# P times V in the attention stage: 16 products of 128 rows and 130 columns in place of 32 of 64 rows and 65 columns

## The chip, the cores and the metric

The kernel runs on one core of one Trainium2 chip. The metric is the time of one execution on the device, in microseconds (us), and the median of several runs is compared. All inputs lie in the device's memory (HBM) when it starts. Host work that lays the arrays out beforehand (`layout`) is not timed.

## The reference

Two stages run one after the other. First comes windowed attention over 8 batches, 8 heads, 576 positions and head size 64. Heads 0 to 3 see the last 32 positions; heads 4 to 7 see every fourth of the last 128:

```python
scores = np.where(masks[None], scale * np.matmul(q, k.transpose(0, 1, 3, 2)), -1e9)
attn = np.exp(scores - np.max(scores, axis=-1, keepdims=True))
attn = attn / (np.sum(attn, axis=-1, keepdims=True) + 1e-09)
attn_out = np.matmul(attn, v)
```

Its output, as 4608 tokens of 512 numbers, goes into a mixture of 16 experts in 4 groups of 4. Each token picks its group by the largest group logit and then its expert by the largest logit within the group, and gets `g_w * e_w * (relu(x @ w1[e]) @ w2[e])`.

## The kernel before

**Attention.** The positions are cut into blocks of 64, and two batches go together: a step `n` (0 to 35, constant `NT`) is one block of all 8 heads of two batches. The dilated heads are sorted by position modulo 4 beforehand, so that each 32 queries see only their own and the previous 32 keys, whatever the head. A step has 8 slots `bb*4 + c` (batch `bb`, head group `c`), each with two head parities or kinds `w`, and two query halves `a`. So one step holds 16 small attentions of 64 queries.

The loop `for s in range(NT + 3)` (L899) is a pipeline: iteration `s` has on TensorE (PE) `scores(s)` (one product with the mask at L263, then 16 products q times k at L275), `transpose_p(s-1)` (four transposes of the probabilities, L298), `av(s-2)` (P times V, L308) and `transpose_x(s-3)` (L360). VectorE (DVE) does the maximum (L285), the subtraction (L286), the reciprocal (L334) and the normalisation (L336). ScalarE (ACT) does the exponential (L291) and the copies out of PSUM (L299, L362, L364). The order on PE, ACT, DVE and SP (the queue that issues the loads and stores) is the order in which the code calls them (`tc.manual_schedule`, L898); GpSimd (POOL) is placed by the framework. The loads run ahead: q and k four steps, v three steps (L920 to L922). Into the same loop the routing of finished batch pairs (`route`, L367), the loads and splits of expert weights (`run(wq)`, L945) and, in the last iterations, early work of the experts are woven, so many pieces per iteration by a budget (`spend`, L250).

**P times V before** (`av`, L301). After the transpose, `pt` holds for each `c` the 128 rows (w, key): rows 0 to 63 belong to `w = 0`, rows 64 to 127 to `w = 1`. For each `c`, `w`, `bb`, `a` one product takes 64 rows of `pt` (32 columns, the queries) and 64 rows of V (65 columns: 64 values and a constant that gives the sum of the probabilities): 32 products of a 64-row, 32-column tile of the array. In the profile each float32 product appears as two matrix instructions and two weight loads, so a step shows 64 pairs. For `a = 1` V is read from `vt` (as loaded), for `a = 0` from `vs`, a copy that `shift_v` (L123) makes on POOL: all of `vt[n]`, then the 32 rows at 0 and at 64 from the block before, three instructions of 520 columns. `vt` and `vs` are rotating buffers of one pool (NV = 5, NVS = 4), 2,080 bytes per partition each; a load of V is one DMA of 128 rows (L121).

**After attention** the pools of it are closed (`att.close()`, L954), and the tiles of the second weight set (`wb`), the expert inputs and others take their place in SBUF and wait for whatever lay there. From then on the experts' two layers (L759, L818) run over 16 experts.

The functions that the change touches, and what calls them:

Of the kernel before, what the change touches and what calls it, by code (L numbers as in the profile page):

```python
# [8 lines left out]
F32 = mybir.dt.float32  # L9
# [3 lines left out]
AF = mybir.ActivationFunctionType  # L13
ALU = mybir.AluOpType
# [3 lines left out]
P = 128  # L18
B, H, S, D = 8, 8, 576, 64
# [5 lines left out]
NJ = S // 64  # L25
NT = NBP * NJ
# [4 lines left out]
SCALE = 0.125  # L31
# [17 lines left out]
NQ, NK, NV, NVS, NPT = 4, 6, 5, 4, 2  # L49
# [15 lines left out]
def moe_attention_kernel(ctx, tc, q, k, v, cmask, wgate, wpack, out):  # L65
    nc = tc.nc
# [11 lines left out]
    id32 = cp.tile([P, P], F32, name="id32")  # L78
# [16 lines left out]
    att = ExitStack()  # L95
    apool = lambda name, bufs=1, **kw: att.enter_context(tc.tile_pool(name=name, bufs=bufs, **kw))
    psA = apool("psA", 1, space=PSUM)
    vp = apool("vp", NV)
    qp = apool("qp", NQ)
    kr = apool("kp").tile([P, 2, 2 * NK, 8, 32], F32, name="kr")  # L100
    pt = [apool(f"pt{i}").tile([P, 4, P], F32, name=f"pt{i}") for i in range(NPT)]
    qb, vt, vs, st, dd, oo, dn = {}, {}, {}, {}, {}, {}, {}
# [14 lines left out]

    def load_v(n):
        if n < NT:
            vt[n] = vp.tile([P, 8, 65], F32, name="vt")  # L120
            nc.sync.dma_start(vt[n], v[n])  # L121

    def shift_v(n):  # L123
        vs[n] = vp.tile([P, 8, 65], F32, name="vs", bufs=NVS)
        nc.gpsimd.tensor_scalar(vs[n], vt[n], 1.0, 1.0, ALU.mult, ALU.mult)
        for r in range(2):
            odd = slice(64 * r, 64 * r + 32)
            if n % NJ == 0:
                nc.gpsimd.memset(vs[n][odd], 0.0)
            else:  # L130
                nc.gpsimd.tensor_scalar(vs[n][odd], vt[n - 1][odd], 1.0, 1.0, ALU.mult, ALU.mult)

    nc.vector.memset(kr[:, :, 0 : NK + 1 : NK], 0.0)
    nc.sync.dma_start(masks[:, 0:2], cm[:, 0:2])
# [7 lines left out]
    load_k(1, 1, 1)  # L142
    load_q(1)
    load_v(0)
    nc.sync.dma_start(masks[:, 2:], cm[:, 2:])
    load_k(2, 0)
    load_k(2, 1)
    load_q(2)
    load_v(1)
    load_q(3)  # L150
    load_v(2)

    ones = cp.tile([P, P], BF16, name="ones")
# [63 lines left out]
    ap = apool("ap", 3)  # L217
# [69 lines left out]
        dd[n] = d  # L287

    def softexp(n):
        p = ap.tile([P, 8, 64], F32, name="p", bufs=2)  # L290
        nc.scalar.activation(p, dd.pop(n), AF.Exp, scale=SCALE)  # L291
        st[n] = p

    def transpose_p(n):
        p = st.pop(n)
        t = psT.tile([P, 4, P], F32, name="t", tag="t")
        for c in range(4):
            nc.tensor.transpose(t[:, c, :], p[:, 2 * c : 2 * c + 2, :].rearrange("p a b -> p (a b)"), id32)  # L298
        nc.scalar.copy(pt[n % NPT], t)  # L299

    def av(n):  # L301
        o = psA.tile([P, 2, 512], F32, name="o", tag="o")
        for c in range(4):
            for w in range(2):
                for bb in range(2):
                    for a in range(2):
                        j = bb * 2 + a
                        nc.tensor.matmul(  # L308
                            o[32 * j : 32 * j + 32, w, c * 65 : c * 65 + 65],
                            pt[n % NPT][64 * w : 64 * w + 64, c, 32 * j : 32 * j + 32],  # L310
                            (vs, vt)[a][n][64 * w : 64 * w + 64, bb * 4 + c, :],
                            start=True,
                            stop=True,
                        )
        oo[n] = o
        den = ap.tile([P, 2, 4], F32, name="den")
        ov = o[:, :, 0:260].rearrange("p k (s c) -> p k s c", c=65)
        nc.scalar.activation(den, ov[:, :, :, 64], AF.Copy, bias=1e-9 / SX)
        dn[n] = den
# [10 lines left out]
    def normalise(n):  # L330
        o = oo.pop(n)
        ov = o[:, :, 0:260].rearrange("p k (s c) -> p k s c", c=65)
        den = dn.pop(n)
        nc.vector.reciprocal(den, den)  # L334
        x = ap.tile([P, 4, 2, 64], F32, name="x", bufs=5)
        nc.vector.tensor_tensor(  # L336
            x.rearrange("p s w c -> p w s c"),
            ov[:, :, :, 0:64],
            den.unsqueeze(3).broadcast_to([P, 2, 4, 64]),
            ALU.mult,  # L340
        )
        st[n] = x
# [549 lines left out]

    start = []
    shift_v(0)
    shift_v(1)
    man = ExitStack()
    ET = mybir.EngineType
    man.enter_context(tc.manual_schedule(engines={ET.PE, ET.Activation, ET.DVE, ET.SP}))  # L898
    for s in range(NT + 3):  # L899
# [3 lines left out]
        if 0 <= s - 1 < NT:  # L903
            transpose_p(s - 1)
        if 0 <= s - 2 < NT:
            av(s - 2)
        if s < NT:
            softexp(s)
        if 0 <= s - 2 < NT:
            if ripe:  # L910
                gate.clear()
            normalise(s - 2)
        if start:
            n = start.pop()
# [13 lines left out]
        if s + 2 < NT:  # L928
            shift_v(s + 2)
# [219 lines left out]
def layout(q, k, v, moe_w_group, moe_w_expert, moe_w1, moe_w2):  # L1149
    import ml_dtypes  # L1150
    import numpy as np

    def seqs(a):
        a = np.asarray(a)
        d = a[:, 4:].reshape(B, 4, CLS, 4, D).transpose(0, 1, 3, 2, 4).reshape(B, 4, S, D)
        return np.stack([a[:, :4], d], axis=1).reshape(NBP, 2, 2, 2, 2, S, D)

    qs, ks, vs = seqs(q), seqs(k), seqs(v)
    qa = qs.reshape(NBP, 2, 2, 2, 2, 3, 3, 2, 32, D)
    qa = qa.transpose(0, 5, 6, 9, 4, 1, 2, 3, 7, 8).reshape(NT, P, 512)  # L1160
    kpad = np.concatenate([np.zeros_like(ks[..., :32, :]), ks], axis=-2).reshape(*ks.shape[:5], 19, 32, D)
    kg = [kpad[..., [2 * j + 2, 2 * j + 1], :, :] for j in range(NJ)]
    ka = np.stack([a.transpose(0, 4, 7, 5, 1, 2, 3, 6) for a in kg], axis=1).reshape(NT // 2, 2, 2, 64, 2, 256)
    ka = ka.transpose(0, 2, 3, 4, 1, 5).reshape(NT // 2, 2, 64, 1024)
    vw = vs.reshape(NBP, 2, 2, 2, 2, 3, 3, 2, 32, D)[..., ::-1, :, :]
    va = vw.transpose(0, 5, 6, 4, 7, 8, 1, 2, 3, 9).reshape(NT, P, 8, D)
    va = np.concatenate([va, np.full_like(va[..., :1], 1.0 / SX)], axis=-1)

    cmask = np.full((2, 2, 32, len(MASKS), 2, 64), -1e9, np.float32)
    for mi, J in enumerate(MASKS):  # L1170
        for a in range(2):
            for qq in range(32):
                i = 64 * J + 32 * a + qq
                for kd in range(2):
                    start = 0 if kd == 0 else (i // CLS) * CLS
                    for kk in range(64):
                        half = (1 - a) * (kk // 32 - 1) - a * (kk // 32)
                        j = i - qq + 32 * half + kk % 32
                        if 0 <= i - j < 32 and j >= start:
                            cmask[:, a, qq, mi, kd, kk] = 0.0  # L1180
    cmask = cmask.reshape(P, -1).astype(ml_dtypes.bfloat16)
    wg = np.concatenate([np.asarray(moe_w_group), np.asarray(moe_w_expert).transpose(1, 0, 2).reshape(DM, 16)], axis=1)
    wg = np.concatenate([wg, np.zeros((DM, 12), wg.dtype)], axis=1)
    wgate = wg.reshape(4, P, 32).transpose(1, 0, 2).reshape(P, -1)
    tok = np.arange(NTOK).reshape(NCHK, P).T
    row = tok // S * S + tok % S % 4 * CLS + tok % S // 4
    pair = 2.0 * (row - PAIR2 // 2 * (tok // (PAIR2 // 2) + 1))
    wgate = np.concatenate([wgate, 2.0 * (row - NTOK), pair], axis=1).astype(np.float32)
    w1 = np.asarray(moe_w1).reshape(NE, 4, P, FF).transpose(0, 2, 1, 3).reshape(NE, P, 4 * FF)
    w2 = np.asarray(moe_w2).reshape(NE, 8, P, DM).transpose(0, 2, 1, 3).reshape(NE, P, 8 * DM)  # L1190
    wpack = np.concatenate([w1, w2], axis=2).reshape(NE * P, 8192)
    c = np.ascontiguousarray
    return dict(q=c(qa), k=c(ka), v=c(va), cmask=c(cmask), wgate=c(wgate), wpack=c(wpack))
# [21 lines left out]
```

## Time and profile before

| | us |
|---|---|
| median of 3 runs | 597.36 |
| lowest and highest run | 597.07, 603.14 |
| the profiled execution, its own time | 598.75 |
| its span, first to last instruction | 597.0 |

The profile holds one execution. Its first part gives the busy time of each engine over the span: PE 561.4 us, its weight loads (PEld) 393.8, DVE 389.5, ACT 326.4, POOL 241.9. Shares over the whole span mix two stages: up to about 172 us the attention steps run, and from about 194 us to the end the experts alone. Matrix instructions overlap in the array and their ends are modelled, so the start of the next group tells more of the pace than a duration does. "Issue" as a releaser means that an engine waited for nothing that the profile shows. Queue q8 and q14 carry the engines' own instructions.

### The profile page before, as it was taken

The page shows a single profiled execution, that of the slowest core. Times are in us where ns is not written, and L with a number is a line of the kernel's source. Part 1 is how long each engine was busy: PE and PEld are TensorE (multiplying, and loading weights), DVE is VectorE, ACT ScalarE, POOL GpSimd, SP SyncE. Part 2 cuts the span into 40 slices and gives each one's busy share as a digit, 9 for nine tenths or more (in the row PEclk, how much of TensorE's full clock was granted, in tenths as well). Part 3 has the DMA queues.
Part 4 walks back from the last instruction along what each step waited for, and adds up shares of the span by engine and source line. Part 5 has one row for each costly group of instructions (what it writes and reads, how often), then busy time and mean ns, then how long its engine had stood idle before and what let it go on. Part 6 is the DMA issues. An engine that isn't in the chain of part 4 may idle for free.

```text
span 597.0 us, 18617 instructions
## 1 busy us (share of the span) xinstructions
PE 561.4 (94%) x7588; PEld 393.8 (66%) x7588; DVE 389.5 (65%) x804; ACT 326.4 (55%) x650; POOL 241.9 (41%) x313
## 2 busy tenths in 40 slices
PE   5888989889698999999999999999999999999995
PEld 3665767566485757765657566666767757767873
DVE  5664876988957833784778695565745766766720
ACT  2554665775555624774455546455655755656521
POOL 4644473636714605161415153442623503423411
PEclk9999999989999999999999999999999999999998
DMA  7998797898473227885677576756867578777300
GB/s 227 307 287 259 230 288 243 285 368 293 99 262 104 80 66 280 284 262 164 198 207 240 176 236 193 223 182 212 250 220 240 197 219 287 234 242 247 94 28 31
DMA packets 48313, 127.52 MB, mean 214 GB/s; under 512 B 7629, under 2 KB 8531, under 8 KB 48226
## 3 DMA queue, kind: packets, MB, share of 16 engines
q1 hardware_dynamic: 40466, 105.33, 55.8%
q0 software_dynamic: 7760, 20.99, 10.2%
q8 instruction: 61, 1.00, 0.7%
q14 instruction: 26, 0.21, 0.1%
HBM read 107.40 MB, written 19.22 MB: 212 GB/s over the span
## 4 chain that ended last, share of the span: by engine, by line
PE 67%; issue 3%; DVE 2%; ACT 1%; POOL 0%; POOLq 0%; ACTq 0%
PE y L818 32%; PE a L759 31%; PE pt L740 3%; DVE mv L505 1%; PE lt_ps L377 0%; PE tx L360 0%; PE o L308 0%; POOL out L779 0%; PE rp L685 0%; PE tb_ps L524 0%; DVE wb1l L641 0%; PE t L298 0%; ACT wb1h L644 0%; ACT room L766 0%; ACT off L243 0%
## 5 line engine op out<-in xcount | busy, mean ns | idle before, releaser
L709 POOL DMA_INDIRECT xr<-xd,sent x80 | 94.5, 1181 | 33.7 <-issue 21.8
L818 PEld LDWEIGHTS <-hh 128*128 128x128 f16 (+14 forms) x960 | 67.3, 99 | 57.6 <-issue 2.5
L779 POOL DMA_INDIRECT out<-yr,sent x30 | 31.0, 1032 | 179.2 <-ACT yr L792 152.7
L767 DVE SCALAR_TENSOR_TENSOR hl<-a,hh 128x256 f16<-128x256 f32 (+14 forms) x136 | 57.1, 422 | 64.1 <-ACT hh L766 64.0
L766 ACT ACTIVATE hh<-a 128x256 f16<-128x256 f32 (+14 forms) x136 | 51.7, 385 | 50.3 <-PE a L759 49.7
L759 PE MATMUL a<-xh,wb1h 128*128 128x256 f16 (+7 forms) x288 | 76.6, 270 | 0.0
L759 PE MATMUL a<-xh,wb1l 128*128 128x256 f16 (+7 forms) x288 | 76.5, 269 | 0.0
L759 PE MATMUL a<-xl,wb1h 128*128 128x256 f16 (+7 forms) x288 | 76.5, 269 | 0.0
L742 DVE TENSOR_TENSOR xl<-pt,xh 128x512 f16<-128x512 f32 (+14 forms) x42 | 24.6, 590 | 73.9 <-ACT xh L741 73.9
L759 PE MATMUL a<-xh,wa1h 128*128 128x186 f16 (+7 forms) x256 | 70.8, 277 | 0.0
L759 PE MATMUL a<-xl,wa1h 128*128 128x186 f16 (+7 forms) x256 | 70.7, 277 | 0.0
L759 PE MATMUL a<-xh,wa1l 128*128 128x186 f16 (+7 forms) x256 | 70.7, 277 | 0.0
L792 ACT ACTIVATE yr<-y,cs 128x512 f32<-128x512 f32 (+4 forms) x30 | 20.7, 688 | 88.7 <-PE y L818 59.5
L759 PEld LDWEIGHTS <-wa1h 128*128 128x128 f16 x640 | 59.0, 98 | 11.5 <-issue 0.3
L759 PEld LDWEIGHTS <-wb1h 128*128 128x128 f16 x576 | 54.3, 98 | 9.6 <-issue 0.2
L818 PE MATMUL y<-wb2h,hh 128*128 128x512 f16 (+7 forms) x272 | 59.7, 305 | 0.0
L818 PE MATMUL y<-wb2l,hh 128*128 128x512 f16 (+7 forms) x272 | 59.5, 304 | 0.0
L818 PE MATMUL y<-wb2h,hl 128*128 128x512 f16 (+7 forms) x272 | 59.5, 304 | 0.0
L818 PE MATMUL y<-wa2h,hh 128*128 128x512 f16 (+7 forms) x208 | 56.8, 331 | 0.0
L818 PE MATMUL y<-wa2h,hl 128*128 128x512 f16 (+7 forms) x208 | 56.6, 330 | 0.0
L818 PE MATMUL y<-wa2l,hh 128*128 128x512 f16 (+7 forms) x208 | 56.6, 330 | 0.0
L818 PEld LDWEIGHTS <-hl 128*128 128x128 f16 (+14 forms) x480 | 34.4, 99 | 25.1
(190 smaller groups left out, 1227.8 us busy)
## 6 DMA issues: line engine op xcount, KB each, us to landing
w<-wpack SPq DMA_DIRECT2D x128, 512.0 KB, 4.8
vt<-v SPq DMA_DIRECT2D x36, 260.0 KB, 4.7
qb<-q SPq DMA_DIRECT2D x36, 256.0 KB, 4.7
xd<-x SPq DMA_DIRECT2D x72, 128.0 KB, 4.2
kr<-k SPq DMA_DIRECT2D x34, 256.0 KB, 5.1
xr<-xd,sent POOLq DMA_INDIRECT x80, 4.5
kr<-k SPq DMA_DIRECT2D x4, 128.0 KB, 3.0
out<-yr,sent POOLq DMA_INDIRECT x30, 3.8
```

The lines of the kernel that those rows point to most:

```text
L505: nc.vector.scalar_tensor_tensor(mv[:, t], high.rearrange("p e k -> p (e k)").unsqueeze(1).broadcast_to([P, 4, NE * NK4]), hl[:, 1, t0 + t ...
L709: nc.gpsimd.indirect_dma_start(out=xr[:, 256 * h : 256 * h + 256], out_offset=None, in_=xd[0:known].rearrange("n (h c) -> (n h) c", h=2), ...
L740: nc.tensor.transpose(pt[:, c, 0:n], xr[0:n, c * P : c * P + P], id32[0:n, 0:n])
L742: nc.vector.tensor_tensor(xl[:, :, t * P : t * P + n], pt[:, :, 0:n], xh[:, :, t * P : t * P + n], ALU.subtract)
L759: nc.tensor.matmul(a[:, 0:cap], ww[:, c * FF + f * P : c * FF + f * P + P], xx[:, c, 0:cap], start=(i == 0), stop=(i == len(mm) - 1),)
L766: nc.scalar.activation(hh[:, f, 0:cap], a[:, 0:cap], AF.Relu)
L767: nc.vector.scalar_tensor_tensor(hl[:, f, 0:cap], a[:, 0:cap], 0.0, hh[:, f, 0:cap], ALU.max, ALU.subtract)
L779: ins = nc.gpsimd.indirect_dma_start(out=out.rearrange("n (g c) -> (n g) c", g=g), out_offset=bass.IndirectOffsetOnAxis(ap=at, axis=0), in ...
L792: nc.scalar.activation(yr[0:n, :], yp[0:n, :], AF.Copy, scale=cs[0:n, t : t + 1])
L818: nc.tensor.matmul(yp[P // g * j : P // g * j + n, 0 : DM // g], h[:, f, t * P : t * P + n], ww[:, f * DM + DM // g * j : f * DM + DM // g ...
```

## The change

- The probabilities are written by `softexp` with the two `w` interleaved (`[P, 4, 64, 2]`), so that after the transpose row `2*key + w` of `pt` belongs to parity `w`.
- V lies in fixed tiles of 128 rows and 2 x 520 columns. Half `w` holds values on the rows of parity `w` alone; the other rows of that half are zero. Zeros are written once per `vt` tile, by an ACT instruction of 1,040 columns; `vs` takes them over with its copies.
- `load_v` issues two DMAs, one per parity, of 64 rows each, in place of one of 128 rows. The bytes are the same.
- `shift_v` issues two POOL instructions of 64 rows and 1,040 columns in place of one of 128 rows and two of 32 rows, of 520 columns each.
- `av` issues 16 products of 128 rows, 32 columns and 130 moving columns (65 per parity).
- PSUM's layout of the output, and the view through which `normalise` writes it, follow; the host's layout of V follows.

```diff
--- before.py
+++ after.py
@@ -95,7 +95,7 @@
     att = ExitStack()
     apool = lambda name, bufs=1, **kw: att.enter_context(tc.tile_pool(name=name, bufs=bufs, **kw))
     psA = apool("psA", 1, space=PSUM)
-    vp = apool("vp", NV)
+    vp = [[apool(f"v{k}{i}").tile([P, 2, 520], F32, name=f"v{k}{i}") for i in range(n)] for k, n in enumerate((NV, NVS))]
     qp = apool("qp", NQ)
     kr = apool("kp").tile([P, 2, 2 * NK, 8, 32], F32, name="kr")
     pt = [apool(f"pt{i}").tile([P, 4, P], F32, name=f"pt{i}") for i in range(NPT)]
@@ -117,18 +117,22 @@
 
     def load_v(n):
         if n < NT:
-            vt[n] = vp.tile([P, 8, 65], F32, name="vt")
-            nc.sync.dma_start(vt[n], v[n])
+            vt[n] = vp[0][n % NV]
+            if n < NV:
+                nc.scalar.activation(
+                    vt[n].rearrange("p w n -> p (w n)"), id32[:, 0:1].broadcast_to([P, 1040]), AF.Copy, scale=0.0
+                )
+            for w in range(2):
+                nc.sync.dma_start(vt[n][w:P:2, w], v[n, w:P:2].rearrange("p s c -> p (s c)"))
 
     def shift_v(n):
-        vs[n] = vp.tile([P, 8, 65], F32, name="vs", bufs=NVS)
-        nc.gpsimd.tensor_scalar(vs[n], vt[n], 1.0, 1.0, ALU.mult, ALU.mult)
-        for r in range(2):
-            odd = slice(64 * r, 64 * r + 32)
-            if n % NJ == 0:
-                nc.gpsimd.memset(vs[n][odd], 0.0)
-            else:
-                nc.gpsimd.tensor_scalar(vs[n][odd], vt[n - 1][odd], 1.0, 1.0, ALU.mult, ALU.mult)
+        vs[n] = vp[1][n % NVS]
+        odd, even = slice(0, 64), slice(64, P)
+        nc.gpsimd.tensor_scalar(vs[n][even], vt[n][even], 1.0, 1.0, ALU.mult, ALU.mult)
+        if n % NJ == 0:
+            nc.gpsimd.memset(vs[n][odd], 0.0)
+        else:
+            nc.gpsimd.tensor_scalar(vs[n][odd], vt[n - 1][odd], 1.0, 1.0, ALU.mult, ALU.mult)
 
     nc.vector.memset(kr[:, :, 0 : NK + 1 : NK], 0.0)
     nc.sync.dma_start(masks[:, 0:2], cm[:, 0:2])
@@ -287,31 +291,32 @@
         dd[n] = d
 
     def softexp(n):
-        p = ap.tile([P, 8, 64], F32, name="p", bufs=2)
-        nc.scalar.activation(p, dd.pop(n), AF.Exp, scale=SCALE)
+        p = ap.tile([P, 4, 64, 2], F32, name="p", bufs=2)
+        d = dd.pop(n).rearrange("p (c w) k -> p c w k", w=2)
+        nc.scalar.activation(p.rearrange("p c k w -> p c w k"), d, AF.Exp, scale=SCALE)
         st[n] = p
 
     def transpose_p(n):
         p = st.pop(n)
         t = psT.tile([P, 4, P], F32, name="t", tag="t")
         for c in range(4):
-            nc.tensor.transpose(t[:, c, :], p[:, 2 * c : 2 * c + 2, :].rearrange("p a b -> p (a b)"), id32)
+            nc.tensor.transpose(t[:, c, :], p[:, c].rearrange("p k w -> p (k w)"), id32)
         nc.scalar.copy(pt[n % NPT], t)
 
     def av(n):
         o = psA.tile([P, 2, 512], F32, name="o", tag="o")
         for c in range(4):
-            for w in range(2):
-                for bb in range(2):
-                    for a in range(2):
-                        j = bb * 2 + a
-                        nc.tensor.matmul(
-                            o[32 * j : 32 * j + 32, w, c * 65 : c * 65 + 65],
-                            pt[n % NPT][64 * w : 64 * w + 64, c, 32 * j : 32 * j + 32],
-                            (vs, vt)[a][n][64 * w : 64 * w + 64, bb * 4 + c, :],
-                            start=True,
-                            stop=True,
-                        )
+            for bb in range(2):
+                for a in range(2):
+                    j = bb * 2 + a
+                    vv = (vs, vt)[a][n].rearrange("p w (s c) -> p w s c", c=65)
+                    nc.tensor.matmul(
+                        o[32 * j : 32 * j + 32, c // 2, c % 2 * 130 : c % 2 * 130 + 130],
+                        pt[n % NPT][:, c, 32 * j : 32 * j + 32],
+                        vv[:, :, bb * 4 + c],
+                        start=True,
+                        stop=True,
+                    )
         oo[n] = o
         den = ap.tile([P, 2, 4], F32, name="den")
         ov = o[:, :, 0:260].rearrange("p k (s c) -> p k s c", c=65)
@@ -334,7 +339,7 @@
         nc.vector.reciprocal(den, den)
         x = ap.tile([P, 4, 2, 64], F32, name="x", bufs=5)
         nc.vector.tensor_tensor(
-            x.rearrange("p s w c -> p w s c"),
+            x.rearrange("p (k s) w c -> p k (s w) c", k=2),
             ov[:, :, :, 0:64],
             den.unsqueeze(3).broadcast_to([P, 2, 4, 64]),
             ALU.mult,
@@ -1163,7 +1168,7 @@
     ka = np.stack([a.transpose(0, 4, 7, 5, 1, 2, 3, 6) for a in kg], axis=1).reshape(NT // 2, 2, 2, 64, 2, 256)
     ka = ka.transpose(0, 2, 3, 4, 1, 5).reshape(NT // 2, 2, 64, 1024)
     vw = vs.reshape(NBP, 2, 2, 2, 2, 3, 3, 2, 32, D)[..., ::-1, :, :]
-    va = vw.transpose(0, 5, 6, 4, 7, 8, 1, 2, 3, 9).reshape(NT, P, 8, D)
+    va = vw.transpose(0, 5, 6, 7, 8, 4, 1, 2, 3, 9).reshape(NT, P, 8, D)
     va = np.concatenate([va, np.full_like(va[..., :1], 1.0 / SX)], axis=-1)
 
     cmask = np.full((2, 2, 32, len(MASKS), 2, 64), -1e9, np.float32)
```

## Rows read from the trace of the kernel before

**Rows 1.** The page: busy time (instructions); instruction queue (packets, MB, share).

```profile
PE 561.4 (94%) x7588; PEld 393.8 (66%) x7588; DVE 389.5 (65%) x804; ACT 326.4 (55%) x650; POOL 241.9 (41%) x313
...
q8 instruction: 61, 1.00, 0.7%
```

**Rows 2.** Windows: bounds, length, PE, PEld, DVE, ACT, POOL, clock, DMA, GB/s.

```profile
16.83:52.53 35.70, 30.40 (x951) 22.20 (x946) 21.87 (x64) 18.60 (x48) 19.54 (x33) 1.00 0.91 288
52.53:104.06 51.53, 48.34 (x1376) 36.00 (x1374) 36.85 (x77) 31.16 (x80) 27.04 (x51) 1.00 0.82 251
104.06:131.77 27.71, 23.16 (x650) 17.02 (x648) 24.96 (x51) 20.80 (x51) 15.26 (x26) 0.94 0.93 319
131.77:172.00 40.23, 33.09 (x883) 24.95 (x880) 32.44 (x73) 25.05 (x65) 22.40 (x33) 0.96 0.71 223
194.00:597.00 403.00, 396.90 (x3350) 271.86 (x3346) 248.90 (x480) 214.65 (x370) 139.07 (x123) 1.00 0.61 196
```

**Rows 3.** Timeline of PE in one undisturbed step: start, us, instruction.

```profile
18.16 0.66 PE L298 MATMUL t<-id,p 128*128 128x128 f32 x4
...
18.75 0.24 PE L308 MATMUL o<-vs,pt 64*32 64x65 f32 x1
...
19.54 0.66 PE L360 MATMUL tx<-id,x 128*128 128x128 f32 x4
...
20.34 1.08 PE L275 MATMUL s<-kr,qb 128*32 128x128 f32 x32
21.35 0.33 PE L298 MATMUL t<-id,p 128*128 128x128 f32 x1
```

**Rows 4.** Busy time, columns as before, from one stall's end to the next's.

```profile
32.42:38.37 5.95, 4.10 (x127) 3.06 (x126) 2.28 (x4) 2.31 (x7) 1.86 (x3) 1.00 0.93 305
```

**Rows 5.** PE's waits, 52.53 to 104.06, then 131.77 to 172: total, times, longest.

```profile
PE o L308 <- issue: 1.8, 3, 1.1
...
PE t L298 <- ACT p L291: 6.3, 4, 2.6
```

**Rows 6.** Issues on SP (ns min/median/max), and the page's time to landing.

```profile
L349 SPq DMA_DIRECT2D xd<-x x72: 445/507/2172, 18.2 to 170.9; - x72
...
L121 SPq DMA_DIRECT2D vt<-v x36: 328/526/1446, 5.2 to 146.9; - x36
...
qb<-q SPq DMA_DIRECT2D x36, 256.0 KB, 4.7
```

**Rows 7.** POOL: the copies' durations (ns min/median/max), and two memsets in the timeline.

```profile
L131 POOL TENSOR_SCALAR vs<-vt x64: 616/619/1697, 14.3 to 160.5; 32x520 f32<-32x520 f32 x64
...
0.80 0.20 POOL masks.py:197 MEMSET id<- 128x128 f32 x1 [0.29 <-POOLq L1205]
...
9.95 0.52 POOL L208 MEMSET xe<- 128x512 f32 x1
```

**Rows 8.** DVE's L505: its group to 260 us, its durations; then DVE beside POOL.

```profile
L505 DVE SCALAR_TENSOR_TENSOR mv<-high,hl,parts 128x256 f16<-128x256 f32 x27 | 15.3, 607 | 0.1
...
L505 DVE SCALAR_TENSOR_TENSOR mv<-high,hl,parts x27: 474/486/926, 72.3 to 192.8; 128x256 f16<-128x256 f32 x27
...
116.41 1.60 POOL L131 TENSOR_SCALAR vs<-vt 32x520 f32<-32x520 f32 x2
...
117.05 1.23 DVE L505 SCALAR_TENSOR_TENSOR mv<-high,hl,parts 128x256 f16<-128x256 f32 x2
```

**Rows 9.** ACT's copies by shape: count | busy us, mean ns | idle before.

```profile
L364 ACT COPY xT<-tx 128x256 f32<-128x256 f32 x23 | 15.0, 651 | 0.0
L362 ACT COPY xT<-tx 128x256 f32<-128x256 f32 x35 | 12.7, 363 | 5.2 <-PE tx L360 5.2
```

**Rows 10.** Timeline at the start; then P times V alone near the end.

```profile
9.09 0.63 ACT L291 ACTIVATE p<-d 128x512 f32<-128x512 f32 x1 [6.80 <-DVE d L286]
...
12.92 1.93 PE L275 MATMUL s<-kr,qb 128*32 128x128 f32 x32 [0.75 <-DMA qb<-q]
...
164.40:165.80 1.40, 1.19 (x64) 0.95 (x64) 0.50 1.03 395
```

## The prediction

> **What bounds the kernel now.** I read the page first, then busy time by stretch, then the timeline of single steps. The page shows PE busy for 94% of the span [rows 1], which hides two stages. From 194 us to the end PE is busy for 396.9 of 403 us with the experts alone [rows 2]; the change does not touch that, so what the attention steps gain or lose reaches the end unchanged. The question is what sets each stretch before it. I cut the stretches at step starts: 16.83 to 52.53 holds 9 steps, then 12 with more routing, then 6 with weight loads, then the rest [rows 2].
>
> An undisturbed step takes 21.35 - 18.16 = 3.19 us on PE [rows 3]. The first 9 steps took 35.70 us, 3.97 each: 7.0 us more than 9 x 3.19. Between the ends of two stalls PE ran 127 products and 126 weight loads [rows 4]. The instruction queue brought 1.00 MB in 61 packets for PE's 15,176 instructions [rows 1], 249 per packet. So I read the stalls that the profile calls "issue" [rows 5] as PE waiting for its next packet of instructions, every 127 pairs. The longest cycle among those I looked at, from one stall's end to the next, is 5.95 us [rows 4].
>
> From 104.06 to 131.77 another engine sets the pace: DVE is busy for 24.96 of 27.71 us, PE for 23.16 [rows 2]. PE's stalls there are largely hidden behind DVE's list of work. After 131.77 PE waits 6.3 us for the exponential [rows 5], which comes behind DVE too.
>
> **The change, part by part.** The sum is made against the profiled span of 597.0 us (597.36 is the runs' median, the execution itself took 598.75); I carry the difference over to the median.
>
> *The products.* P times V occupies PE from 18.75 to the next group at 19.54: 0.79 us for 64 pairs, eight array tiles side by side. The new products have the shape of the scores, 128 rows by 32 columns, with 130 moving columns in place of 128, 32 pairs. The scores take 21.35 - 20.34 = 1.01 us [rows 3], so 1.01 x 130/128 = 1.03. I take +0.24 us per step, as this row has nearly the same instruction. Ends: at today's 12.3 ns per pair it would be 0.39 (-0.40 per step); with twice today's time 1.58 (+0.79).
>
> The Trainium skill ("TensorEngine Tiling (Array Packing)", section Theoretical Speedup) gives two-fold row tiling as worth up to 2x where at most 64 rows are contracted, which speaks against giving it up. The scores' row does not bear out the whole factor: today's products do not reach what eight tiles would allow.
>
> *Instruction fetches.* A step issues 105 pairs now and 73 after it. So 127 pairs last 1.74 steps of 3.43 us, 5.97 us, just above the longest cycle of 5.95. I let the stalls vanish; the case in which they only become rarer is a rival.
>
> *The 9 steps to 52.53.* PE alone would need 9 x 3.43 = 30.9 us, 4.8 less. But the DMA engines are busy for 0.91 of 35.70 us = 32.5 us [rows 2] and the bytes stay, so I take -3.2.
>
> *The 12 steps to 104.06.* PE sets them (48.34 of 51.53). Products +2.9. The waits inside P times V are 1.8 us in 3 stalls [rows 5]; they count from a product's modelled end, about 0.2 us after the next could start, so 2.4. Sum +0.5.
>
> *The 6 steps to 131.77.* Between DVE's 51 instructions some 0.03 us each can't go, so of its 2.75 idle us 1.2 are there to gain: -1.2, whatever PE saves. The longer products are covered by PE's 4.5 idle us there; were that cover gone, they would cost 1.4.
>
> *The last steps.* The 6.3 us of waits for the exponential cover +0.24 in most. The last two P times V stand behind them. At the half clock today's takes 1.19 us [rows 10]; a score group took 1.93 in that state [rows 10] against 1.08, so +0.85 for one and +0.24 for the other: +1.1.
>
> *V's loads.* One more issue on SP per step. A store of 64 rows is the nearest, 0.51 us median; the load of 128 rows it replaces cost 0.53 [rows 6]; ends 0.33 and 0.6. Behind the second half on SP stand the store of x, the next q and k, and the weight loads. If SP falls behind by 0.5 us per step, 9 steps make 4.5 us; a load of q is issued four steps before its use (13.7 us) and lands after 4.7 [rows 6], so 9 us cover it, and the slower steps after 52.53 let SP catch up. Zero there. At the start nothing covers it: PE waits 0.75 us for q before the third step [rows 10], and half a V load now stands ahead of it: +0.5. The first P times V falls into the clock's slow start (scores 1.93 us [rows 10]): +0.9. Start: +1.4.
>
> *Zeros.* Five ACT instructions of 1,040 columns, once, each at most twice the 0.63 us that 512 took. Three lie in ACT's idle 6.80 us before the first exponential [rows 10]; two follow the first two exponentials, where the copies behind them wait for PE. Zero; without that cover 2.5 us. A V load waits for its zeros, and q, k and stores wait behind it on SP, by less than one instruction.
>
> *POOL's copies.* Three of 0.62 us become two of 1,040 columns. Memsets of 128 and 512 columns took 0.20 and 0.52 us [rows 7], 0.83 ns per column, so about 0.62 + 520 x 0.83 ns = 1.05 us each: 2.1 in place of 1.86 per step; ends 1.24 (no growth) and 2.48 (double). POOL has 15.26 busy of 27.71 us [rows 2], so it is not late itself. But DVE seems to pay: L505's mean is 607 ns and its minimum 474 [rows 8], and the pair at 117.05 overlaps a copy [rows 8]. 27 x 133 ns = 3.6 us. Chance of meeting a copy grows by 2.1/1.86 = 1.13, the rest to wait for by 1.05/0.62 = 1.7, together 1.9: +3.2; ends x0.67 (-1.2) and x2.65 (+5.9). I take +2.5, as some of it falls where PE sets the pace.
>
> *The exponential's spaced writes.* 256 columns written at a spacing of four numbers took 651 ns, without spacing 363 [rows 9]. At a spacing of two no row exists: 0 to 1.13 ns x 512 = 0.58 us per step. In the 9 fast steps 0.6 us lie between the exponential's end and its transpose, in the 6 steps ACT has 6.9 idle us [rows 2]; only at the 4 longest waits of the last steps would it show, 2.3 us. I take 0.
>
> The Trainium skill ("SBUF — State Buffer", Specifications) states full bandwidth from two hits per 16-byte line on; by that a spacing of two numbers costs nothing and one of four does, as the copies' rows show. The sum would be the same.
>
> *The rest.* The normalisation's order, DVE's reads and the tiles that later take V's place cost nothing: the same elements, and the experts' weights are written after the last P times V. If that cover went, the first expert would wait for V's last reader.
>
> Sum: -3.2 + 0.5 - 1.2 + 1.1 + 1.4 + 2.5 = **+1.1 us**, or 598.5.
>
> **The rivals.**
> 1. *Fetch stalls stay and only become rarer* (slower). If a fetch is slow because the DMA engines are full, a longer block does not help. Then 0.7 of the stalls stay: the 9 steps give 2.2 - 0.3 x 7.0 = 0, the 12 steps 2.9 - 0.7 = +2.2. With the other terms +6.0, 603.4. For it: DMA share 0.91. Against: the longest cycle is below the new block. It decides where a fetch takes more than 5.97 us. 0.14.
> 2. *Products take twice today's time* (the rule above). +0.79 each: 9 steps +0.1, 12 steps +7.1, 6 steps -1.2, last two +1.9, start +1.4, copies +2.5: +11.8, 609. Against it stands the scores' row. 0.04.
> 3. *DVE waits for the longer copies at their worst*: +5.9 in place of +2.5, 602. 0.10.
> 4. *Products are as cheap per pair as today's*: 9 steps -3.2, 12 steps -7.2, 6 steps -1.2, the last steps -0.8, start +0.5, copies -1.2: -13, 584. The scores' row is against it. 0.08.
> 5. *The 6 steps give PE's stalls back in full* (about 4.3 us) and POOL's copies do not grow: -3.2 + 0.5 - 4.3 + 1.1 + 1.4 - 1.2 = -5.7, 591.7. DVE's busy share speaks against it. 0.08.
>
> My forecast has 0.56. It is the likeliest: **598.5 us**. About 1% (6 us: below 591.4, above 603.3) is what a measurement of this kernel can tell from no change. Faster: rival 4 and half of 5, with a little more for the forecast's tail, 0.14. Slower: half of rival 1, rival 2, and tails of 3 and the forecast, 0.16. The range 591.5 to 604 leaves out rivals 2 and 4 and the edges of 1 and 5, about 0.2.
>
> **What the changed profile would show.** P times V from its first product to the next group: 1.03 us, 32 pairs. Stalls called "issue" inside PE's groups nearly gone before 104 us and 52 instruction packets in place of 61 (36 x 64 instructions fewer, 249 in each). The 9 steps shorter by about 3 us, the 12 about as long. DVE still over 90% busy over the 6 steps, L505's mean above 607 ns. POOL's copies near 1.05 us; the exponential still 0.63. The forecast fails if the stalls stay, if P times V is far from 1.03, or if the 6 steps shorten by more than DVE's idle time.

## The result, and the profile after

The changed kernel took 607.94 us (median of 4 runs, 604.93 to 609.75), beside it the kernel before 600.25 us (median of 4, 597.07 to 604.87). The ratio is **1.0107, with a 95% interval of 1.0058 to 1.0156**: slower by about 6.4 us by the ratio (7.7 by the two medians), where 598.5 us and no measurable change had been forecast. The profiled execution took 604.93 us with a span of 602.9 us, against 598.75 and 597.0 before: 5.9 us to be found.

The page after (busy time of each engine, then the instruction queue) answers to [rows 1]:

```profile
PE 564.9 (94%) x6436; PEld 397.2 (66%) x6436; DVE 396.5 (66%) x804; ACT 332.3 (55%) x655; POOL 250.6 (42%) x277
...
q8 instruction: 52, 0.85, 0.6%
```

PE executes 1,152 matrix instructions fewer (two for each of 16 products in 36 steps), and 52 packets of instructions are fetched, not 61. DVE executes the same 804 instructions, but takes 7.0 us more for them.

Busy time by stretch, cut at the same steps as [rows 2] (bounds, length, then busy time with the number of instructions for PE, PEld, DVE, ACT and POOL, then granted clock, DMA share, GB/s):

```profile
16.04:50.93 34.89, 31.42 (x661) 23.14 (x658) 23.51 (x64) 18.93 (x48) 21.27 (x21) 1.00 0.84 258
50.93:104.01 53.08, 49.73 (x992) 37.60 (x990) 37.22 (x78) 31.85 (x81) 32.11 (x43) 1.00 0.83 252
104.01:133.65 29.64, 24.49 (x459) 17.96 (x456) 25.84 (x46) 20.32 (x50) 19.32 (x21) 0.88 0.88 280
133.65:178.00 44.35, 35.84 (x632) 27.28 (x630) 36.64 (x77) 26.13 (x67) 21.88 (x26) 0.92 0.74 242
```

The start is 0.8 us shorter, the 9 steps 0.8 us shorter, the 12 steps 1.55 us longer, the 6 steps 1.9 us longer. From there to the last group of routing it is 4.1 us more (49.58 against 45.51), and the experts after that are unchanged (419.7 in both). So the loss lies after 50.93 us, and mostly after 104 us.

PE's waits, 16 to 175 us (total, times, longest), first of the kernel after, then of the kernel before:

```profile
PE t L303 <- ACT p L296: 9.8, 8, 3.6
PE s L279 <- DMA kr<-k: 8.4, 6, 2.3
```

```profile
PE o L308 <- issue: 9.3, 10, 1.7
PE t L298 <- ACT p L291: 7.3, 6, 2.6
PE s L275 <- issue: 2.3, 3, 1.9
```

Here the main exchange is to be seen: the 9.3 + 2.3 = 11.6 us of waits called "issue", which the prediction read as waits for instructions, are gone from the attention, and PE waits for k instead, which it did not do before. ACT has a new late load as well, the expert's weights, in the list of its waits:

```profile
ACT wa1h L649 <- DMA w<-wpack: 5.2, 3, 3.0
```

The timeline of PE in the 6 steps (start, busy time, instruction, idle time before it) shows what such a late load sets off:

```profile
119.81 0.66 PE L303 MATMUL t<-id,p 128*128 128x128 f32 x4 [3.60 <-ACT p L296]
120.40 1.59 PE L313 MATMUL o<-v,pt 128*32 128x130 f32 x32
...
124.54 0.87 PE L279 MATMUL s<-kr,qb 128*32 128x128 f32 x12 [1.08 <-DMA kr<-k]
```

After 3.60 us of idle time PE's next products are slow, 1.59 us in place of 1.03. The granted clock was 1.00 up to there, and is 0.61 on the mean from there to 126 us, between its two levels of 1.2 and 2.4 GHz (the last number but two here, columns as above):

```profile
119.81:126.00 6.19, 5.11 (x69) 3.73 (x73) 5.86 (x9) 4.79 (x13) 2.74 (x3) 0.61 0.98 329
```

Over the 6 steps it is 0.88, against 0.94 before.

The reason that the loads are late stands in the timeline of SP, the engine that issues them:

```profile
30.47 0.53 SPq L107 DMA_DIRECT2D qb<-q  x1
31.05 0.59 SPq L116 DMA_DIRECT2D kr<-k  x1
31.75 1.18 SPq L126 DMA_DIRECT2D v<-v  x2
33.05 1.15 SPq L354 DMA_DIRECT2D xd<-x  x2
34.31 0.91 SPq L107 DMA_DIRECT2D qb<-q  x1
```

Six issues follow each other without a pause; from one q to the next is 34.31 - 30.47 = 3.84 us. Nine times that is 34.6 us, and the 9 steps took 34.89. Added up over the trace, gaps of more than 0.2 us between SP's issues come to 0.4 us in the 9 steps and 0.4 us in the 12 (2.7 and 12.4 us before). With five issues, in the kernel before, a round of SP took as little as 29.75 - 26.65 = 3.10 us, just below PE's undisturbed step of 3.19:

```profile
26.65 1.09 SPq L349 DMA_DIRECT2D xd<-x  x2
27.83 0.54 SPq L107 DMA_DIRECT2D qb<-q  x1
28.42 0.59 SPq L116 DMA_DIRECT2D kr<-k  x1
29.11 0.55 SPq L121 DMA_DIRECT2D vt<-v  x1
29.75 1.54 SPq L349 DMA_DIRECT2D xd<-x  x2
```

After the change PE's undisturbed step is shorter than SP's round, 3.44 us, from the first row here to the last:

```profile
16.04 0.39 PE L267 MATMUL s<-masks,idb 128*128 128x512 bf16 x1
...
17.96 1.09 PE L313 MATMUL o<-v,pt 128*32 128x130 f32 x32
18.98 0.66 PE L365 MATMUL tx<-id,x 128*128 128x128 f32 x4
19.48 0.38 PE L267 MATMUL s<-masks,idb 128*128 128x512 bf16 x1
```

**The theories** that the runs were to tell apart: S, the sixth issue per step keeps SP busy without a pause, so that k and the weights come late; L, DVE waits for POOL's longer copies. The expectations also name T, the products' +0.24 us per step, and D, the half loads of V themselves land late because the DMA engines are full. What L takes is counted in the traces as DVE's excess: over DVE's instructions in which one of POOL's copies ends, the time that each takes above the shortest of its line and shape (less than 0.08 us left out). All ratios below are to the kernel before, with 95% intervals.

### The profile page after: what moved, and what is told of

The parts are those of the page before. It is cut to its first block, busy times and chain, and to the rows that moved or that the text cites. A ratio compares the mean times of both kernels' runs of the same rounds, so it can differ in the third digit from the quotient of the medians.

```text
span 602.9 us, 16374 instructions
## 1 busy us (share of the span) xinstructions
PE 564.9 (94%) x6436; PEld 397.2 (66%) x6436; DVE 396.5 (66%) x804; ACT 332.3 (55%) x655; POOL 250.6 (42%) x277
## 4 chain that ended last, share of the span: by engine, by line
PE 65%; issue 3%; ACT 2%; DVE 1%; POOL 1%; POOLq 0%; ACTq 0%
PE y L823 31%; PE a L764 30%; PE pt L745 3%; POOL xe L714 1%; DVE mv L510 1%; ACT off L247 1%; POOL out L784 0%; PE rp L690 0%; PE tb_ps L529 0%; ACT ohl L248 0%; ACT xT L369 0%; PE o L313 0%; ACT room L771 0%; PE lt_ps L382 0%; DVE room L772 0%
## 5 line engine op out<-in xcount | busy, mean ns | idle before, releaser
L131 POOL TENSOR_SCALAR v<-v 64x1040 f32<-64x1040 f32 x36 | 39.1, 1086 | 40.5 <-DMA v<-v 30.7
```

The lines of the kernel that those rows point to most:

```text
L131: nc.gpsimd.tensor_scalar(vs[n][even], vt[n][even], 1.0, 1.0, ALU.mult, ALU.mult)
```

## Experiments

**The extra issue alone, and the longer copies alone, on the kernel before.** First b_split, which loads V as before, but in two issues:

```
-            nc.sync.dma_start(vt[n], v[n])
+            for w in range(2):
+                nc.sync.dma_start(vt[n][w:P:2], v[n, w:P:2])
```

> The kernel before, with V's load cut into two DMAs of 64 rows (even rows, odd rows), the same bytes, products and copies as before. S: one more issue per step takes SP to about 4 us per step, ratio 1.005 to 1.015 (3 to 9 us). L and T: no change, 0.998 to 1.002.

Measured: 609.87 us, 1.0151 [1.0108, 1.0195]. One more issue per step, with the same bytes, products and copies, costs no less than the whole change did (the two intervals overlap). PE's waits, 16 to 175 us, show the same late k:

```profile
PE s L276 <- DMA kr<-k: 13.4, 8, 3.5
PE t L299 <- ACT p L292: 7.0, 5, 3.8
PE o L309 <- issue: 2.9, 4, 1.3
```

SP's gaps over 0.2 us come to 0.5 and 0.4 us in the 9 and 12 steps, as in the kernel after. So one more issue per step, in the form of two half loads, is enough for the loss; whether the issue costs it or the half loads do (D) is for a_qv to tell. The Trainium skill ("DMA: Bandwidth & Descriptors", section Rules for kernel authors) advises one transfer of 128 partitions over two to disjoint halves, as both use the same DMA engines; the ratio agrees with the advice, but the trace shows SP's issues to be what fills up.

Second b_wide, which copies each V row twice over, so that POOL's three copies per step have 1,040 columns:

```
...
+        both = vp.tile([P, 2, 520], F32, name="vs", bufs=NVS)
+        nc.gpsimd.tensor_scalar(both, twice(vt[n], slice(0, P)), 1.0, 1.0, ALU.mult, ALU.mult)
...
+                nc.gpsimd.tensor_scalar(both[odd], twice(vt[n - 1], odd), 1.0, 1.0, ALU.mult, ALU.mult)
```

> The kernel before, with POOL's three copies per step widened to 1,040 columns (the second 520 are not used); loads and products as before. L: copies of 1.05 us in place of 0.62, time of DVE lost to them 5.6 x 1.69 x 1.7 = 16 us, about 8 of it where DVE sets the pace, ratio 1.007 to 1.015. S and T: no change, 0.998 to 1.002.

Measured: 606.65 us, 1.0105 [1.0059, 1.0150]. DVE's excess is 15.4 us; 5.6 in the kernel before. PE waits for it through ACT's exponential (its waits, 16 to 175 us):

```profile
PE t L300 <- ACT p L293: 12.0, 9, 4.2
PE o L310 <- issue: 7.8, 9, 1.9
```

For the copies themselves PE waits only 1.0 us. So L is a cost of its own, for three long copies per step, where SP has five issues. In the changed kernel, with two, the excess is 10.7 us.

**Back to five issues, in the changed kernel.** a_qv keeps everything of the change but the separate load of q. From the third step on q lies between V's two halves, in the tile and in the array that the host lays out, so each half of V comes with q's rows of its parity, in two DMAs of 64 rows and 1,040 columns; the ring has six tiles in place of five, and V is issued four steps ahead, not three:

```
-            qb[n] = qp.tile([P, 512], F32, name="qb")
-            nc.sync.dma_start(qb[n], q[n])
+            t = vp[0][n % NV]
+            qb[n], vt[n] = t[:, 1, 0:512], t[:, 0:3:2]
...
+            flat = t.rearrange("p w c -> p (w c)")
+            for w in range(2):
+                nc.sync.dma_start(flat[w:P:2, 520 * w : 520 * w + 1040], v[n, w:P:2])
```

> The changed kernel with q and V in one array: each of the two DMAs per step takes V's half and q of 64 rows (from the third step on), so that SP has five issues per step as before the change, all of 64 rows but k's; bytes +0.8%. S (SP's issues): PE's waits for k and ACT's for the weights nearly gone, 5 to 11 us below the changed kernel, ratio to before 0.992 to 1.002. D (the DMA engines are full, so half loads land late): as the changed kernel, 1.010. L (POOL's copies): 1.010.

Measured: 597.68 us, **0.9958 [0.9930, 0.9986]**. PE's waits for k are down to 4.7 us, and ACT's wait for the weights from 5.2 to 0.4:

```profile
PE t L309 <- ACT p L302: 9.7, 9, 2.2
PE s L285 <- DMA kr<-k: 4.7, 4, 1.9
```

SP's round of five issues is 34.55 - 31.32 = 3.23 us, below PE's 3.44 again:

```profile
31.32 1.19 SPq L360 DMA_DIRECT2D xd<-x  x2
32.62 1.19 SPq L114 DMA_DIRECT2D v<-v  x2
33.85 0.60 SPq L126 DMA_DIRECT2D kr<-k  x1
34.55 2.44 SPq L360 DMA_DIRECT2D xd<-x  x2
```

The profiled span is 596.7 us, 6.2 less than the changed kernel's; 3.1 of these come after the 6 steps (46.45 against 49.58), where PE no longer waits for k at all. V's loads are still of 64 rows, the products are the same, and DVE's excess is still 8.6 us, so neither D nor T nor L by itself is the cause of the loss. S is confirmed from this side: without its sixth issue the change is slightly faster than the kernel before. (V's earlier issue and the sixth tile came with this edit. They do not bring forward k, for which PE waited.)

**Shorter copies on top.** a_qv_cut also cuts each of POOL's copies in two of 520 columns, the same work in shorter pieces:

```
+        for w in range(2):
+            nc.gpsimd.tensor_scalar(vs[n][even, w], vt[n][even, w], 1.0, 1.0, ALU.mult, ALU.mult)
...
+                nc.gpsimd.tensor_scalar(vs[n][odd, w], vt[n - 1][odd, w], 1.0, 1.0, ALU.mult, ALU.mult)
```

> As the changed kernel with q and V in one array, and each POOL copy cut into two of 520 columns. L: DVE's time lost to copies falls from about 10 to about 7 us, ratio 1 to 4 us below that kernel. S alone: the same as that kernel. If the copies' total time counts and not their length, a little slower, as POOL copies for 2.5 us per step in place of 2.1.

Measured: 595.60 us, **0.9923 [0.9895, 0.9950]**, the best of all versions. DVE's excess beside the copies falls from 8.6 to 6.6 us, and the span by 2.3. The intervals of a_qv and a_qv_cut overlap, but they share the spread of the kernel before. Set directly against each other, 12 runs each, the means differ by 2.0 us, with a 95% interval of 0.7 to 3.4: once SP is not late, shorter copies pay, as L had it. The first three stretches of a_qv_cut, columns as above:

```profile
18.34:50.45 32.11, 31.15 (x661) 22.98 (x658) 22.24 (x64) 18.79 (x48) 24.59 (x42) 0.99 0.89 280
50.45:102.19 51.74, 49.68 (x992) 37.58 (x990) 37.45 (x78) 31.84 (x81) 36.10 (x67) 1.00 0.85 266
102.19:128.45 26.26, 22.15 (x459) 16.22 (x456) 24.40 (x48) 20.22 (x50) 20.99 (x33) 1.00 0.95 320
```

The 6 steps take 26.26 us at full clock, not 29.64 at 0.88, and the 9 steps 32.11: PE, busy for 31.15 of it, now sets them.

**Shorter copies alone.** a_cut makes the same cut in the changed kernel, with its six issues.

> The changed kernel, V still loaded in two issues per step; each of POOL's two copies of 1,040 columns is cut into two of 520. Theory S with L (the extra issue on SP and the copies' lock on DVE both cost): the excess of DVE's instructions over their shortest goes from 10.7 us to about 8, the steps before 104 us stay where SP sets them (34.9 and 53.1 us), the 6 steps and the last ones give back about 2 us: ratio to the kernel before 1.004 to 1.009. Theory S alone (DVE's excess is covered by waits for late loads): no change from the changed kernel, 1.009 to 1.012. Theory L alone (the issue costs nothing): back to about the kernel before, 0.998 to 1.002.

Measured: 607.73 us, 1.0104 [1.0065, 1.0143], the changed kernel's own ratio. DVE's excess fell to 8.1 us and its busy time to 392.1 us, yet nothing is seen of it in the time. PE's waits, 16 to 175 us, suggest why:

```profile
PE t L304 <- ACT p L297: 8.9, 5, 2.9
PE s L280 <- DMA kr<-k: 6.6, 4, 3.9
PE s L280 <- DMA v<-v: 5.7, 5, 2.2
```

Loads are as late as before the cut, 12.3 us of waits together (the last row's wait is put down to V, though the scores read q and k alone). The ratio lies where S alone had it (1.009 to 1.012), though its interval does not shut out S with L (1.004 to 1.009). So the reading is that the lock on DVE is covered as long as SP is late; a gain of some 2 us would not have been seen.

**Five issues by a merged store.** a_merge stores the two blocks of x in one DMA, whose destination has an outermost dimension of 2.

```
...
-            nc.sync.dma_start(xd[row : row + 64], x[64 * bb : 64 * bb + 64].rearrange("p s w c -> p (s w c)"))
+        to = xd[2 * bp * S : 2 * bp * S + 2 * S].rearrange("(b s) c -> b s c", b=2)[:, 64 * J : 64 * J + 64]
+        nc.sync.dma_start(to, x.rearrange("p s w c -> p (s w c)"))
```

> The changed kernel, with the two stores of x per step (64 rows each) issued as one DMA of 128 rows, so that SP has five issues per step again, as before the change. Theory S (SP issues back to back, 3.85 us per step, falls behind, and k and the weights come late): PE's waits for k (8.4 us) and ACT's for the weights (5.2 us) go, ratio to the kernel before 0.985 to 1.000. Theory L (POOL's longer copies hold up DVE, 10.7 us in place of 5.6): no change, 1.010 as the changed kernel. Theory T (the products' +0.24 us per step is all of it): no change, 1.010.

Measured: 688.11 us, 1.1449 [1.1401, 1.1497]. A miss, and no test of S: the issue behind the merged store, on SP's timeline, takes 3.51 us where it took 0.53.

```profile
30.75 0.55 SPq L353 DMA_DIRECT2D xd<-x  x1
31.39 3.51 SPq L107 DMA_DIRECT2D qb<-q  x1
```

A rule that fits is in the Trainium skill ("DMA: Bandwidth & Descriptors", section Rules for kernel authors): a DMA whose outermost dimension is smaller than 16 runs on no more engines than that dimension counts. The trace agrees in its direction, 3.5 us and 14% of the time; no row shows how many engines the store ran on.

a_merge_cut is the same with the copies cut.

> The changed kernel with one store of x per step and each POOL copy cut into two of 520 columns (four of 0.62 us in place of two of 1.05). S with L: below the one with the merged store alone by 1 to 3 us, since the rest of a copy that DVE waits for shrinks by 0.6 and the share of time that POOL copies grows by 1.18. S alone: as the one with the merged store. T: 1.010.

Measured: 687.90 us, 1.1447 [1.1399, 1.1496]. The store covers whatever the cut does.

**One issue moved to ACT's queue.** a_act issues V's second half there.

```
-                nc.sync.dma_start(vt[n][w:P:2, w], v[n, w:P:2].rearrange("p s c -> p (s c)"))
+                (nc.sync, nc.scalar)[w].dma_start(vt[n][w:P:2, w], v[n, w:P:2].rearrange("p s c -> p (s c)"))
```

> The changed kernel with the second DMA of each V load issued from ACT's queue; the same DMAs otherwise. S: SP is back to five issues, waits for k and the weights go, but ACT gives some 0.5 us per step to the issue; ratio 0.994 to 1.004. D: the same transfers on the same DMA engines, so as the changed kernel, 1.010. L: 1.010.

Measured: 613.50 us, 1.0205 [1.0149, 1.0261]: a miss for S as I had put it. SP did get free time (gaps over 0.2 us of 5.9 and 13.6 us in the 9 and 12 steps), but by the profile it spent it waiting (SP's waits, 16 to 175 us):

```profile
SPq L354 <- DMA v<-v: 21.8, 15, 3.8
SPq L126 <- DMA v<-v: 5.9, 4, 1.9
```

Its stores of x now wait for a V load to land, and q and k stand behind them; PE's waits for k are 11.9 us. The freed issue was replaced by a wait between two queues, so this run does not count against S, nor for it. Which ordering makes the store wait for a V load is not settled.

**Fewer issues in the kernel before.** b_qv puts q and V into one DMA of 128 rows there, four issues per step.

```
-            qb[n] = qp.tile([P, 512], F32, name="qb")
-            nc.sync.dma_start(qb[n], q[n])
+            t = vp.tile([P, 1032], F32, name="vt")
+            qb[n], vt[n] = t[:, 520:1032], t[:, 0:520].rearrange("p (s c) -> p s c", c=65)
...
+                nc.sync.dma_start(t, v[n])
```

> The kernel before with q and V of a step in one DMA of 128 rows (from the third step on): four issues per step instead of five; products, copies and bytes as before. S: SP was busy for nine tenths of the first stretch even before, but was seldom waited for; 0.990 to 1.000. D and L: 0.998 to 1.002. PE's instruction stalls should stay.

Measured: 605.89 us, 1.0069 [1.0036, 1.0102]: a miss. PE's waits, 16 to 175 us:

```profile
PE o L310 <- issue: 14.6, 9, 3.1
PE t L300 <- ACT p L293: 4.5, 3, 2.0
PE s L277 <- issue: 3.3, 4, 1.0
```

The waits for instructions grew from 11.6 to 17.9 us, and a load of k took 7.0 us from issue to landing, 5.1 before (medians, here of only 3 loads out of 34, those whose landing the profile could tell). With four issues SP puts its loads on the queues sooner, and PE's packets of instructions, which come over the same DMA engines, seem to wait behind them; that reading is argued, not shown. It would explain why five issues pay in the changed kernel, which needs a packet only every 1.74 steps, and four do not in the kernel before.

## Why the prediction was wrong

**The step that failed is "V's loads".** It priced the extra issue at 0.5 us per step, let SP fall behind by 4.5 us in the 9 steps, and then took zero, because q is issued four steps ahead and "the slower steps after 52.53 let SP catch up". The lag came, but it was not repaid, and q was not the load to count it for.
- SP was nearly full already. Its round of back-to-back issues went from 3.10 to 3.84 us, 0.74 and not 0.5 more, past PE's 3.44. Five issues left it 2.7 us of gaps in the 9 steps and 12.4 us in the 12; six leave 0.4 and 0.4. It did not catch up in the 12 steps: its 75 issues there, eight of them longer than 0.7 us (9.2 us together; what held those up the profile does not settle), filled the 53.08 us, where PE was busy for 49.73. Where the 12 steps begin, q had been issued 12.9 us ahead of its step before and 6.5 us ahead after; where they end, 14.5 and 9.8. A lead in steps covers a lag that is repaid; here most of it stayed.
- The lead was counted for q, whose waits the trace of before showed. For q it was long enough: from 16 us on PE never waited for it. The load that came late was k, 8.4 us of waits. Its two halves are issued in alternate steps, and the half issued in odd steps is first used three steps later, not four. All of PE's waits for loads fall into such later steps (4, 8, 10, 12, 20, 28 and 30). This half's issue ended 6.0 to 11.3 us ahead of its step before, and 0.4 to 6.3 us after.
- Behind V on the same queue stand the weights. That was said, but not priced: ACT waited for them 5.2 us, and PE with it 3.60 us at 119.81, after which its clock fell.

The term was worth 6 to 9 us: 6.2 by the spans of the changed kernel and a_qv, 8.9 by their ratios, 9 by b_split (0.0151 x 600). Without its sixth issue the change came to 0.9958 x 597.36 = 594.9 us, inside the range given.

**The rest of the sum, part by part.**
- *Products*: forecast 1.03 us for 32 pairs. Measured 18.98 - 17.96 = 1.02. Right.
- *Instruction fetches*: they vanish from the attention, and 52 packets were forecast. Right; rival 1 would have had 0.7 of them stay, so its 603.4 is near the time by another route.
- *The 9 steps*: forecast -3.2 on the ground that DMA engines bound them at 32.5 us. Measured -0.8, since SP set them; in a_qv_cut, where it no longer does, 32.11 us, or -3.6. The size came out, the ground did not: there the DMA engines are busy for 0.89 x 32.11 = 28.6 us and PE for 31.15.
- *The 12 steps*: +0.5 forecast, +1.55 measured with six issues; 51.74 us in a_qv_cut, +0.2.
- *The 6 steps*: -1.2 forecast on the ground that DVE sets them. With late loads +1.9; a_qv_cut gives -1.4 (26.26 against 27.71 from [rows 2]), with DVE busy for 24.40 of 26.26.
- *POOL's copies*: 1.06 us each, 1.05 forecast. The growth of what DVE loses was forecast as a factor of 1.9 and came out as 10.7 / 5.6 = 1.9. The instruction on which it was based [rows 8] went from a mean of 607 to 693 ns:

```profile
L510 DVE SCALAR_TENSOR_TENSOR mv<-high,hl,parts 128x256 f16<-128x256 f32 x27 | 17.7, 693 | 0.1
L510 DVE SCALAR_TENSOR_TENSOR mv<-high,hl,parts x27: 468/480/1731, 72.4 to 198.7; 128x256 f16<-128x256 f32 x27
```

  Its shortest is about the same. The one of 1,731 ns is not a copy's work alone: it starts at 113.58 us, the copy ends at 114.45, and two more POOL instructions (L503) follow it. The next longest take 1,322, 1,276 and 1,265 ns, each beside a copy, where the longest before was 926. But the sum of 3.6 us was of this one line; over all of DVE's lines it was 5.6 and grew by 5.1. The +2.5 was low for the lock and, as a_cut is read above, too high for the time. The Trainium skill ("SBUF — State Buffer", section Who interferes with whom) describes contention between the two engines as an exclusive lock on ports that they share; that the loss grows with the copies' length (5.6 us before, 15.4 with three long copies in b_wide) agrees.
- *The last steps*: forecast +1.1, measured +4.1 to the last group of routing, in which PE waits 2.1 us for k and the clock is at 0.92. In a_qv, with no such wait, it is 46.45 - 45.51 = +0.9. That this is near +1.1 is luck: 0.85 of it was to come from one P times V at the half clock, and there the granted clock is 1.00 and the last ones take 1.09 us.
- *The start*: forecast +1.4, measured -0.8. The lag feared there did build up (the fifth load of q is issued at 12.33 us, 9.78 before), and PE paid for it: ahead of the third step it waits 1.90 us for q, 0.75 before, and ahead of the first P times V 0.85 us for POOL's copy of V. What made up for it was not in the sum: products were fast sooner, the third step's scores in 1.08 us in place of 1.93, and the first P times V in 1.19 against 1.07 before, where +0.9 was forecast. Why is open; the profile's granted clock, 1.00 there in both kernels, does not tell.
- *The exponential*: forecast unchanged. Its median is 672 ns against 631. PE waits for it eight times, so the 41 ns are directly at most 0.3 us of those 9.8:

```profile
L296 ACT ACTIVATE p<-d x36: 657/672/764, 8.9 to 168.5; 128x512 f32<-128x512 f32 x36
```

**Left open**: how the last 4 us divide. b_split loses only 1.0 us after its 6 steps and b_wide 6.0, while a_cut, with less lock, keeps them all; both causes can act there, and each profile is one execution.

## What to carry to other kernels

Count the issuing queue as an engine: its issues per step times their duration, set against the pace at which the kernel is to run, before an extra issue is called hidden. A lead of some steps hides a delay, not a rate, and it must be counted for the load on that queue with the shortest lead. When a faster part moves the bound, look for the resource that was nearly full: here fewer instructions on PE paid only once the sixth issue was off the queue. Fewer issues are no gain by themselves: the kernel before was slower with four than with five.

## What the runs showed of the hardware

- One more issue of 0.6 us per step on a queue that already had five cost 1.5% (b_split), with not a byte more.
- PE's waits called "issue", read as waits for instructions, differ widely with the same 61 packets: 11.6 us before, 3.6 in b_split, whose loads come later, and 17.9 in b_qv, whose loads come sooner. That they depend on what else the DMA engines carry is argued, not shown: in b_split PE also waits 13.4 us for k, in which a packet can arrive. The Trainium skill ("Runtime: NRT & Kernel Launch", section Instruction fetch mechanics) calls the crossing of a block of 256 instructions mostly hidden; the packets' size agrees (249), and by this reading of the 11.6 us they were not hidden here.
- An exponential written at a spacing of two numbers takes 672 ns for 512 columns, 631 without: 7% more, where a spacing of four took 651 in place of 363 [rows 9].
